# Attention by pairs of 64-row matmuls: scores of two key chunks side by side, the second product in two halves

## The chip, the cores and the metric

The kernel runs on one core of a Trainium2 chip. The metric is the device time of one execution in microseconds, the median of several. TensorE (PE in the profile) does the matmuls and loads its weights (PEld) beside them; ScalarE (ACT), VectorE (DVE) and GpSimd (POOL) do the rest of the arithmetic; SyncE (SP) issues most of the DMAs.

## What is computed

Three layers follow each other on 4 sequences of 3072 rows with 256 columns. The change touches the first alone.

```python
scores = (1 / S) * z @ z.T                # z: 3072 x 64 per sequence
attn = np.maximum(scores, 0.0) ** 2
x = u * (attn @ v)                        # v, u: 3072 x 256
h = x @ w_in;  x = (h - np.tanh(h)) @ w_out
k = np.maximum(mix_k(x) @ w_k, 0.0)
out = sigmoid(mix_r(x) @ w_r) * ((k * k) @ w_v)
```

## The kernel before

**Number format.** The matmuls take fp32r, a shortened fp32. Every operand is split into a high part h and the rest l, and a product is made of h·h, h·l and l·h (`PASSES`, line 605).

**Tiles and units.** Attention is cut into 24 tiles of 512 queries (`t`; batch `b` and group `g` are `divmod(t, 6)`). A tile has 12 units, each of two key chunks of 128 keys. A unit's scores go to a work tile `w_A` in PSUM (128 x 2 x 512), ScalarE applies relu (line 632) and square (633) and rounds the result to h (89), VectorE takes the rest l (92), and the second product `acc_A` (line 880) multiplies h and l by v. Since z @ z.T is symmetric, a block of scores that was made in an earlier tile of the same batch is not made again: VectorE turns it (661), SyncE stores it (669, `at`), and it is loaded later (695, `b`) as a reused unit. Of the 288 units 168 are fresh and 120 reused; group 0 has 12 fresh ones per tile, group 5 has two. The table `pairs` (line 647) says in which place of a tile a fresh ("f") and a reused ("r") unit stand.

**Scores.** z has 64 columns and TensorE's contraction has 128 rows. Before, `z1` holds h of z on rows 0 to 63 and l on rows 64 to 127, and `z2` the same two swapped. A chunk's scores are two full matmuls into the same bank: z1 by z1 (h·h + l·l) and z1 by z2 (h·l + l·h). That is 4 matmuls per fresh unit.

**Second product.** Per unit 2 chunks x 2 column halves of v x 3 passes = 12 full matmuls, into two accumulator banks (`acc_A`, 128 x 512 each). Four banks exist with that tag, so two tiles can be under way. At the end of a tile VectorE multiplies each accumulator by u, straight from PSUM (line 1223), and the result is stored to `x1d`.

**Order.** All is written out by hand: unit n's scores, then the second product of unit n - 2 (`LAG` is 2), and so on. Each engine runs its own instructions strictly in the order in which they were written; all work between engines is tied by semaphores. Loads have a unit at which they are issued (`load`), other work (splitting weights, turning u, the multiply by u) is a list of steps that `run_steps` hands out between units, by a budget per unit (line 1394) and a last unit for each. After attention come the two feed-forward layers, which use TensorE with full 128-row matmuls throughout.

The profile names a buffer by its tag: `h_A`, `l_A` are the parts of a fresh unit, `h_t`, `l_t` those of a reused one, `z` is z1, z2 and, in the listings of order, q the queries.

Of the kernel before, what the change touches and what calls it, by code (L numbers as in the profile page):

```python
# [14 lines left out]
P = 128  # L15
# [4 lines left out]
def relu2_attention__tanh_ffn__channel_mix_kernel(  # L20
# [74 lines left out]
    zin, z1, z2, vraw, vs, uin, uT = {}, {}, {}, {}, {}, {}, {}  # L95

    def z_load(b, g):

        if (b, g) == (0, 2):
            t = p4(f"zin{b}_{g}", shape=(P, 32, 32))[:, :16]  # L100
        elif b:
            t = p2(f"zin{b}_{g}", F32R)
        else:
            t = p2(f"zin{b}_{g}").rearrange("p (k i) -> p k i", i=32)
        src = z[b, g * TB : (g + 1) * TB, :].rearrange("(k j) (a i) -> a j k i", j=32, i=32)
        o = t.bitcast(F32).rearrange("p (k i) -> p k i", i=32) if b else t
        for h in range(1 if b else P // DQ):
            for a in range(DQ // 32):
                q = nc.scalar if h and b == 0 and g < 2 else nc.sync
                q.dma_start(out=o[h * DQ + 32 * a : h * DQ + 32 * a + 32], in_=src[a])  # L110
        zin[b, g] = t

    def z_steps(b, g):
        st = {}

        def turn():
            a = zin.pop((b, g))
            st["t"] = t = scratch(f"zt{b}_{g}")[:, 0]
            st["w"] = w = p2(f"z1_{b}_{g}", F32R)
            nc.vector.transpose(out=t, in_=a.rearrange("p k i -> p (k i)"))  # L120

        def high():
            t, w = st["t"], st["w"]
            if b or g < 3:
                nc.vector.tensor_copy(w, t)
            else:
                copy_hi(w, t)
            if b == 0 and g == 0:
                z2[0] = p2("z2_0", F32R)
                copy_hi(z2[0][DQ:], t[DQ:])  # L130

        def low():
            t, w = st["t"], st["w"]
            sub_lo(w[DQ:], t[DQ:], w[DQ:])
            if b == 0 and g == 0:
                sub_lo(z2[0][:DQ], t[:DQ], w[:DQ])
            z1[b, g] = w

        if not b:
            return turn, high, low  # L140

        def half():

            a = zin[b, g]
            t = scratch(f"zt{b}_{g}")[:DQ, 0]
            st["w"] = w = p2(f"z1_{b}_{g}", F32R)
            nc.vector.transpose(out=t, in_=a[:DQ].bitcast(F32))
            nc.vector.tensor_copy(w[:DQ], t)
            sub_lo(a[:DQ], t, w[:DQ])
            z1[b, g] = w  # L150

        return [(1.7, half)]
# [478 lines left out]
    def square(a, w, sc):  # L631
        nc.scalar.activation(out=a, in_=w, func=ACTF.Relu, scale=sc)  # L632
        nc.scalar.activation(out=a, in_=a, func=ACTF.Square)  # L633

    def square_split(name, w, sc, high, beside, a=None):
        a = a or scratch(f"a_{name}")
        h, l = parts(name)
        square(a, w, sc)
# [7 lines left out]
    for g, order in enumerate(  # L646
        ("ffffffffffff", "ffffrfrfffff", "ffrffrffrffr", "frfrfrfrfrfr", "rfrrfrrfrrfr", "rrfrrrrrfrrr")
# [69 lines left out]
    def score(o, t, p, j, k):  # L717
        b, g = divmod(t, NG)
        kp = pairs[g][p]
        kc = kp // 2 * 4 + kp % 2 + 2 * j  # L720
        lhsT = z1[b, kc // 4][:, (kc % 4) * P : (kc % 4 + 1) * P]
        nc.tensor.matmul(o, lhsT, (z2[t], z1[b, g])[not k], start=not k, stop=bool(k))  # L722

    def opening(begin):
# [27 lines left out]
        def scores(n, o):  # L752
            for j in range(2):
                for k in range(2):
                    score(o[j], 0, n, j, k)
# [11 lines left out]
        for n, j, k in (  # L767
            (0, 0, 0), (0, 1, 0), (1, 0, 0), (0, 0, 1), (0, 1, 1), (1, 1, 0), (1, 0, 1), (1, 1, 1)
        ):
            score(o[n][j], 0, n, j, k)  # L770
# [11 lines left out]
        o = single(3)  # L782
        scores(3, o)
# [7 lines left out]
        square(x, w[1], scale)  # L791
        copy_hi(h, x)
# [7 lines left out]
        for n in (2, 3):  # L800
            a[n] = x = wide(n)
            if n == 2:
                square(x, w[2], scale)
                vh[1][0]()
            else:
                for j in range(2):
                    nc.scalar.activation(out=x[:, j], in_=o[j], func=ACTF.Relu, scale=scale)
                nc.scalar.activation(out=x, in_=x, func=ACTF.Square)
                vh[2][0]()
# [7 lines left out]
    def produce(unit):  # L817
# [3 lines left out]
        if n in turned:  # L821
            views, split[unit] = turned.pop(n)
            for hj, lj, xj in views:
                sub_lo(lj, xj, hj)
            return
        w = work(f"w_{name}")
        if kind == "A":
            b, g = divmod(t, NG)
            kp = pairs[g][p]
            for j in range(2):  # L830
                for k in range(2):
                    score(w[:, j], t, p, j, k)
            kept_on = (b, g, kp // 2) in kept

            def beside(a):
                run_steps(n)
                if kept_on and not later(n):
                    keep(n, b, g, kp, a)

            a = wide(n) if later(n) and kept_on else None  # L840
            split[unit] = square_split(
                name, w, scale,
                nc.vector.tensor_copy if not n // NP and n % 2 else copy_hi, beside, a,
            )
            if kept_on and later(n):
                keep(n, b, g, kp, a)

    def get_acc(kind, t):
        if (kind, t) not in acc:
            acc[kind, t] = [  # L850
                ps.tile([P, 512], F32, tag="acc", name=f"acc_{kind}{t}_{c}", bufs=2 * DC)
                for c in range(DC)
# [7 lines left out]
    def pieces_of(unit):  # L860
# [13 lines left out]
        elif unit in units[1 : NP - 1]:  # L874
            q = (0, 1, 2) if unit == units[2] else (0, 2, 1)
            order = [(j, c, n) for n in q for j in range(2) for c in range(DC)]

        def one(j, c, n):
            a, m = PASSES[n]
            nc.tensor.matmul(  # L880
                o[c],
                w[j][a][:, c * P : (c + 1) * P],
                s[m][:, j],
                start=p == 0 and j == 0 and n == 0,
                stop=p == last and j == 1 and n == 2,
            )
# [331 lines left out]

    def x1_steps(t):
        def f():  # L1220
            x, o = uT.pop(t), acc.pop(("A", t))
            for c in range(DC):
                nc.vector.tensor_tensor(out=x[:, c], in0=o[c], in1=x[:, c], op=ALU.mult)
# [33 lines left out]
    for t in range(NT):  # L1257
# [3 lines left out]
        if t:  # L1261
            load(t * NP - 5, z_swap, t)
        if t < NT - 1:
            task(t * NP + NP + LAG, t * NP + NP + LAG + 3, x1_steps, t)
    for b in range(1, B):
# [6 lines left out]
        for g in range(NG):  # L1272
# [3 lines left out]
            load(n + 6, z_below, b, g)  # L1276
# [110 lines left out]
    def run_steps(n):  # L1387
# [21 lines left out]
    with tc.manual_schedule():  # L1409
# [11 lines left out]
        for j in range(10):  # L1421
            for r in (slice(0, DQ), slice(DQ, P)) if 3 < j < 7 else (slice(0, P),):
                nc.tensor.matmul(  # L1423
                    idle[:, bool(r.start) if 3 < j < 7 else j % 2], zeros[r],
                    zeros[r].unsqueeze(1).broadcast_to([r.stop - r.start, 4, P]), start=True, stop=True,
# [87 lines left out]
```

## Time and profile before

| | us |
|---|---|
| median of 3 runs | 2478.32 (2478.29 to 2479.51) |
| the profiled execution | 2478.75 |
| its span, first to last instruction | 2477.0 |
| TensorE busy | 2469.6, 100% |
| VectorE, ScalarE busy | 1955.1 (79%), 1889.0 (76%) |
| second product of attention, share of the chain | 32% |
| scores of attention, share of the chain | 6% |

The span holds 31131 instructions. Times in rows are us from the span's start. A matmul's row gives its length to the last result, and the next one starts before that; the time that a matmul costs is the distance between two starts. In rows of the timeline that stand for several instructions, x2 means that two follow each other in one row with one start and one total length. In the rows of stretches, (x884) is the number of instructions that touch the stretch.

### The profile page before, as it was taken

What the parts mean: (1) busy time and instruction counts of PE and PEld (TensorE: products, weight loads), DVE (VectorE), ACT (ScalarE), POOL (GpSimd) and SP (SyncE); (2) the same over time, 40 slices, a digit from 0 to 9 for tenths busy, and PEclk for the clock granted to TensorE, in tenths of its full rate; (3) what the DMA queues carried; (4) which work ended last, traced back from release to release, by engine and by line L of the source; (5) the groups of instructions that cost most, each with busy time, mean ns of one, the idle gap of its engine ahead of it and who ended that gap; (6) DMA issues with size and microseconds to landing.
All of it is one profiled execution on the core that took longest, in us unless ns stands there. A gap on an engine that the chain in (4) does not pass through costs nothing.

```text
span 2477.0 us, 31131 instructions
## 1 busy us (share of the span) xinstructions
PE 2469.6 (100%) x10873; PEld 2040.1 (82%) x10873; DVE 1955.1 (79%) x2723; ACT 1889.0 (76%) x2516; POOL 242.7 (10%) x314
## 2 busy tenths in 40 slices
PE   9999999999999999999999999999999999999998
PEld 7888888888888888888888888888888888888887
DVE  8887888787888868777777777777778778878877
ACT  8766876787678766777777777778777988888886
POOL 0000000000000000022132222222222000000200
PEclk9999999999999999999999999999999999999999
DMA  7799579768967991155665556545667454445733
GB/s 200 230 224 221 191 209 248 200 198 214 244 191 224 271 231 69 47 109 109 145 134 122 101 111 132 125 96 109 135 127 166 137 128 128 105 125 133 164 106 71
DMA packets 442670, 385.87 MB, mean 156 GB/s; under 512 B 263952, under 2 KB 349968, under 8 KB 442512
## 3 DMA queue, kind: packets, MB, share of 16 engines
q1 hardware_dynamic: 390288, 307.58, 44.0%
q0 software_dynamic: 45888, 75.51, 18.3%
q8 instruction: 85, 1.39, 0.2%
q10 hardware_dynamic: 6336, 0.79, 0.2%
q14 instruction: 73, 0.60, 0.1%
HBM read 226.23 MB, written 199.48 MB: 172 GB/s over the span
## 4 chain that ended last, share of the span: by engine, by line
PE 100%; DVE 0%; issue 0%; POOL 0%; DVEq 0%; POOLq 0%
PE acc_A L880 32%; PE acc_H L936 21%; PE wa L899 16%; PE we L899 12%; PE acc_K L936 10%; PE w_A L722 6%; PE wa_r L899 1%; PE we_q L899 1%; PE we_r L899 0%; PE idle L1423 0%; DVE ot L1211 0%; DVE sg L1202 0%; POOL zeros L1418 0%; DVEq L1202 0%; POOLq L1500 0%
## 5 line engine op out<-in xcount | busy, mean ns | idle before, releaser
L880 PE MATMUL acc_A<-h_A,v 128*128 128x512 f32 x1344 | 433.1, 389 | 0.1
L632 ACT ACTIVATE a_A<-w_A 128x1024 f32<-128x1024 f32 (+1 forms) x168 | 171.6, 1021 | 181.6 <-PE w_A L722 181.3
L880 PE MATMUL acc_A<-h_t,v 128*128 128x512 f32 x960 | 310.0, 389 | 0.0
L880 PEld LDWEIGHTS acc_A<-h_A,v 128*128 128x128 f32 x1344 | 252.1, 188 | 52.7 <-issue 0.5
L936 PE MATMUL acc_H<-h_Hy,w_out 128*128 128x512 f32 x768 | 263.8, 389 | 0.0
L880 PE MATMUL acc_A<-l_A,v 128*128 128x512 f32 x672 | 256.4, 389 | 0.0
L92 DVE TENSOR_TENSOR l_A<-a_A,h_A 128x1024 fp32r<-128x1024 f32 (+1 forms) x169 | 201.3, 1191 | 64.6 <-ACT h_A L89 63.9
L936 PE MATMUL acc_H<-h_Hx,w_out 128*128 128x512 f32 x768 | 252.1, 389 | 0.0
L899 PE MATMUL wa<-xo_T,w_in 128*128 128x512 f32 x864 | 242.8, 389 | 0.0
L661 DVE STREAM_TRANSPOSE k<-a_A 128x512 f32<-128x512 f32 x240 | 156.1, 689 | 78.9 <-ACT a_A L633 78.4
L880 PEld LDWEIGHTS acc_A<-h_t,v 128*128 128x128 f32 x960 | 180.2, 188 | 37.4
L1002 DVE TENSOR_TENSOR r<-we,r 128x512 f32<-128x512 f32 x144 | 99.5, 691 | 126.1 <-PE we L899 84.8
L1162 POOL DMA_DIRECT2D mixd<-far x48 | 48.7, 1014 | 1511.4 <-ACT far L1159 1496.2
L1036 DVE TENSOR_TENSOR rc<-we,rc 128x512 f32<-128x512 f32 x144 | 99.3, 689 | 119.0 <-PE we L899 83.5
L899 PEld LDWEIGHTS wa<-xo_T,w_in 128*128 128x128 f32 x864 | 162.1, 188 | 34.1 <-DVE rc L1036 0.4
L880 PE MATMUL acc_A<-l_t,v 128*128 128x512 f32 x480 | 186.7, 389 | 0.0
L633 ACT ACTIVATE a_A<-a_A 128x1024 f32<-128x1024 f32 (+1 forms) x168 | 177.4, 1056 | 5.3
L92 DVE TENSOR_TENSOR l_Hy<-g_H,h_Hy 128x1024 fp32r<-128x1024 f32 x144 | 175.5, 1219 | 7.3 <-ACT h_Hy L89 4.6
L89 ACT ACTIVATE h_t<-b 128x512 fp32r<-128x512 f32 x240 | 137.1, 619 | 56.1 <-PE acc_A L880 56.1
L92 DVE TENSOR_TENSOR l_Hx<-g_H,h_Hx 128x1024 fp32r<-128x1024 f32 (+1 forms) x145 | 175.3, 1209 | 3.5 <-ACT h_Hx L89 2.5
L909 ACT ACTIVATE g_H<-rc 128x1024 f32<-128x1024 f32 x96 | 101.9, 1061 | 96.4 <-DVE rc L1036 95.4
L89 ACT ACTIVATE h_A<-a_A 128x1024 fp32r<-128x1024 f32 x161 | 170.6, 1060 | 4.6
(254 smaller groups left out, 5744.3 us busy)
## 6 DMA issues: line engine op xcount, KB each, us to landing
at<-k SPq DMA_DIRECT2D x120, 512.0 KB, 3.7
b<-at SPq DMA_DIRECT2D x240, 256.0 KB, 6.5
timed<-mixd POOLq DMA_DIRECT2D x144, 256.0 KB, 5.3
mixd<-own SPq DMA_DIRECT2D x96, 256.0 KB, 2.1
mx_T<-timed SPq DMA_DIRECT2D x96, 256.0 KB, 4.6
mx_B<-mixd SPq DMA_DIRECT2D x72, 256.0 KB, 4.6
uin<-in_u_dram SPq DMA_DIRECT2D x192, 64.0 KB, 2.7
x1d<-uT SPq DMA_DIRECT2D x24, 512.0 KB, 4.6
```

The lines of the kernel that those rows point to most:

```text
L89: nc.scalar.activation(out=o, in_=i, func=ACTF.Copy)
L92: nc.vector.tensor_tensor(out=o, in0=i, in1=hi.bitcast(F32), op=ALU.subtract)
L632: nc.scalar.activation(out=a, in_=w, func=ACTF.Relu, scale=sc)
L633: nc.scalar.activation(out=a, in_=a, func=ACTF.Square)
L661: nc.vector.transpose(out=t[:, :, :, c].rearrange("p b a j -> p a b j"), in_=a[:, c].rearrange("p (a b i) -> p a b i", a=4, b=4),)
L722: nc.tensor.matmul(o, lhsT, (z2[t], z1[b, g])[not k], start=not k, stop=bool(k))
L880: nc.tensor.matmul(o[c], w[j][a][:, c * P : (c + 1) * P], s[m][:, j], start=p == 0 and j == 0 and n == 0, stop=p == last and j == 1 and n ...
L899: nc.tensor.matmul(o, w[l], x[m], start=first and k == 0, stop=last and k == 2, skip_group_check=True,)
L909: nc.scalar.activation(out=g, in_=h, func=ACTF.Tanh)
L936: nc.tensor.matmul(o[c], w[a][:, f % 4, c * P : (c + 1) * P], hp[n, half, t][m], start=bool(first and k == 0), stop=bool(last and k == 2),)
L1002: nc.vector.tensor_tensor(out=r1, in0=e, in1=r1, op=ALU.add)
L1036: nc.vector.tensor_tensor(out=rc[:, k], in0=x, in1=rc[:, k], op=ALU.add)
```

## The change

- Scores take three passes (h·h, h·l, l·h), each of two 64-row matmuls: key chunk j has its 64 columns of z on rows 64 j to 64 j + 63, with its own bank of `w_A`. `keys` holds h and l of a group's keys laid out so, and `asks` the queries with the same 64 columns on both row halves. `ask` fills the queries by eight DMAs from `keys`, where `z_swap` had two; `z_below` is gone.
- The second product goes in 64-row matmuls as well: rows 0 to 63 into accumulators 2 and 3, rows 64 to 127 into accumulators 0 and 1. Only the last two units of attention stay whole. In a tile's first and last unit the column halves follow each other (c outside).
- At the end of a tile `x1_add` copies accumulators 0 and 1 to SBUF on ScalarE and adds 2 and 3 on VectorE, before the multiply by u. For the scores of the unit at that place ScalarE's copies stand behind the relu and behind the square.
- `produce` is split: `scores` ahead of the second product of unit n - 2, the rest behind it. Two rows of `pairs` are rearranged, the budget of `run_steps` is 1.4 lower at the second unit of a tile, and the warm-up matmuls are all halves.

```diff
         def turn():
             a = zin.pop((b, g))
-            st["t"] = t = scratch(f"zt{b}_{g}")[:, 0]
-            st["w"] = w = p2(f"z1_{b}_{g}", F32R)
+            st["t"] = t = scratch(f"zt{b}_{g}")[:, 0, :n]
+            if n == 512:
+                w = asks[0] = [p2(f"q0_{l}", F32R) for l in range(2)]
+            else:
+                w = p2(f"z_{b}_{g}", F32R).rearrange("p (l n) -> p l n", l=2)
+                w = [w[:, l] for l in range(2)]
+            st["w"] = w
...
-    def z_below(b, g):
-        a = zin.pop((b, g))
-        nc.sync.dma_start(out=z1[b, g][DQ:].bitcast(F32), in_=a[:DQ].bitcast(F32))
-
-    def z_swap(t):
+    def ask(t):
+
         b, g = divmod(t, NG)
-        w = p2(f"z2_{t}", F32R)
-        nc.sync.dma_start(out=w[:DQ].bitcast(F32), in_=z1[b, g][DQ:].bitcast(F32))
-        nc.sync.dma_start(out=w[DQ:].bitcast(F32), in_=z1[b, g][:DQ].bitcast(F32))
-        z2[t] = w
+        w = asks[t] = [p2(f"q{t}_{l}", F32R) for l in range(2)]
+        for l in range(2):
+            for d in range(2):
+                for h in range(2):
+                    nc.sync.dma_start(
+                        out=w[l][d * DQ : (d + 1) * DQ, h * 256 : (h + 1) * 256].bitcast(F32),
+                        in_=keys[b, g][l][h * DQ : (h + 1) * DQ].bitcast(F32),
+                    )
...
-    def score(o, t, p, j, k):
+    def score(o, t, p, k):
+
         b, g = divmod(t, NG)
         kp = pairs[g][p]
-        kc = kp // 2 * 4 + kp % 2 + 2 * j
-        lhsT = z1[b, kc // 4][:, (kc % 4) * P : (kc % 4 + 1) * P]
-        nc.tensor.matmul(o, lhsT, (z2[t], z1[b, g])[not k], start=not k, stop=bool(k))
+        for j in range(2):
+            r = slice(j * DQ, (j + 1) * DQ)
+            n = kp % 2 + (2 * j if (b, kp // 2) == (0, 0) else 0)
+            lhsT = keys[b, kp // 2][PASSES[k][0]][r, n * P : (n + 1) * P]
+            nc.tensor.matmul(o[j], lhsT, asks[t][PASSES[k][1]][r], start=k == 0, stop=k == 2)
...
+        elif p in (0, last):
+            order = [(j, c, n) for c in range(DC) for n in range(3) for j in range(2)]
+        whole = at[unit] >= NA - LAG
 
         def one(j, c, n):
+
             a, m = PASSES[n]
-            nc.tensor.matmul(
-                o[c],
-                w[j][a][:, c * P : (c + 1) * P],
-                s[m][:, j],
-                start=p == 0 and j == 0 and n == 0,
-                stop=p == last and j == 1 and n == 2,
-            )
+            for r in (slice(0, P),) if whole else (slice(0, DQ), slice(DQ, P)):
+                nc.tensor.matmul(
+                    o[c if r.start else DC + c],
+                    w[j][a][r, c * P : (c + 1) * P],
+                    s[m][r, j],
...
+    def x1_add(t):
+
+        x = added[t] = scratch(f"xs{t}")
+        o = acc["A", t] if t == NT - 1 else acc.pop(("A", t))
+
+        def one(c):
+            nc.scalar.activation(out=x[:, c], in_=o[c], func=ACTF.Copy)
+            if t < NT - 1:
+                nc.vector.tensor_tensor(out=x[:, c], in0=o[DC + c], in1=x[:, c], op=ALU.add)
+
+        return [lambda c=c: one(c) for c in range(DC)]
...
-            load(t * NP - 5, z_swap, t)
+            load(t * NP - 5, ask, t)
...
+            left -= 1.4 if q == LAG - 1 else 0.0
...
-            produce(units[n])
+            w = scores(units[n])
             consume(units[n - LAG])
+            ends_now = n == NA - 1 or n % NP == LAG - 1 and n > NP
+            produce(units[n], w, x1_add((n - LAG) // NP) if ends_now else ())
```

TensorE at the end of tile 6, before: the scores of unit 1 of tile 7 (`w_A7_1`), then the first six of the twelve matmuls of the last unit of tile 6.

```order
L722 MATMUL w_A7_1_2721<-z1_1_1_1255 128x512
L722 MATMUL w_A7_1_2721<-z2_7_2528,z1_1_1_1255 128x512
L722 MATMUL w_A7_1_2721<-z1_1_1_1255 128x512
L722 MATMUL w_A7_1_2721<-z2_7_2528,z1_1_1_1255 128x512
L880 MATMUL acc_A6_0_2393<-h_A6_11_2661,v1_5_2477 128x512
L880 MATMUL acc_A6_0_2393<-l_A6_11_2662,v1_5_2477 128x512
L880 MATMUL acc_A6_0_2393<-h_A6_11_2661,v1_5_2477 128x512
L880 MATMUL acc_A6_1_2394<-h_A6_11_2661,v1_5_2477 128x512
L880 MATMUL acc_A6_1_2394<-l_A6_11_2662,v1_5_2477 128x512
L880 MATMUL acc_A6_1_2394<-h_A6_11_2661,v1_5_2477 128x512
```

The same place in the changed kernel; the number behind `acc_A6` is the accumulator.

```order
L724 MATMUL w_A7_1_3918<-q7_0_3631,z_1_1_1720 128x512 x2
L724 MATMUL w_A7_1_3918<-q7_1_3632,z_1_1_1720 128x512 x2
L724 MATMUL w_A7_1_3918<-q7_0_3631,z_1_1_1720 128x512 x2
L881 MATMUL acc_A6_2_3413<-h_A6_11_3855,v1_5_3809 128x512
L881 MATMUL acc_A6_0_3411<-h_A6_11_3855,v1_5_3809 128x512
L881 MATMUL acc_A6_2_3413<-h_A6_11_3855,v1_5_3809 128x512
L881 MATMUL acc_A6_0_3411<-h_A6_11_3855,v1_5_3809 128x512
L881 MATMUL acc_A6_2_3413<-l_A6_11_3856,v1_5_3809 128x512
L881 MATMUL acc_A6_0_3411<-l_A6_11_3856,v1_5_3809 128x512
L881 MATMUL acc_A6_2_3413<-l_A6_11_3856,v1_5_3809 128x512
L881 MATMUL acc_A6_0_3411<-l_A6_11_3856,v1_5_3809 128x512
```

Four full score matmuls became three pairs of halves, and each full matmul of the second product a pair that alternates between two accumulators. The listing has 10873 matmuls before and 14648 after.

ScalarE at that place, before: relu, square and rounding of units 1 and 2 of tile 7.

```order
L632 ACTIVATE a_A7_1_2726<-w_A7_1_2721 128x1024
L633 ACTIVATE a_A7_1_2726<-a_A7_1_2726 128x1024
L89 ACTIVATE h_A7_1_2727<-a_A7_1_2726 128x1024
L632 ACTIVATE a_A7_2_2757<-w_A7_2_2752 128x1024
L633 ACTIVATE a_A7_2_2757<-a_A7_2_2757 128x1024
```

In the changed kernel (`xs6` is the SBUF tile that takes tile 6's accumulators):

```order
L627 ACTIVATE a_A7_1_3950<-w_A7_1_3918 128x1024
L1229 ACTIVATE xs6_3949<-acc_A6_0_3411 128x512
L630 ACTIVATE a_A7_1_3950<-a_A7_1_3950 128x1024
L1229 ACTIVATE xs6_3949<-acc_A6_1_3412 128x512
L89 ACTIVATE h_A7_1_3951<-a_A7_1_3950 128x1024
L627 ACTIVATE a_A7_2_3996<-w_A7_2_3961 128x1024
```

Two copies of accumulators now stand between the steps of unit 1; each waits for TensorE's last matmul into its bank, and VectorE's two additions stand behind them on VectorE.

## Rows read from the trace of the kernel before

**Rows 1.** The page: busy time of the engines, and the chain that ended last.

```profile
PE 2469.6 (100%) x10873; PEld 2040.1 (82%) x10873; DVE 1955.1 (79%) x2723; ACT 1889.0 (76%) x2516; POOL 242.7 (10%) x314
PE 100%; DVE 0%; issue 0%; POOL 0%; DVEq 0%; POOLq 0%
```

**Rows 2.** The whole span, matmuls of line 880, then of 722: busy us (xcount).

```profile
0.00:2477.00 2477.00, 811.42 (x3456) 648.25 (x3456) 1.00 0.63 156
...
0.00:2477.00 2477.00, 179.89 (x672) 126.52 (x672) 1.00 0.63 156
```

**Rows 3.** The chain that ended last, in order of time: start us, us.

```profile
207.81 16.32 PE acc_A L880 x72
```

**Rows 4.** Timeline of TensorE's warm-up, six moments, then its weight load: start us, us.

```profile
2.02 0.63 PE L1423 MATMUL idle<-zeros 128*128 128x512 f32 x1
2.44 0.63 PE L1423 MATMUL idle<-zeros 128*128 128x512 f32 x1
3.00 0.79 PE L1423 MATMUL idle<-zeros 64*128 64x512 f32 x2
3.60 0.63 PE L1423 MATMUL idle<-zeros 64*128 64x512 f32 x2
4.02 0.63 PE L1423 MATMUL idle<-zeros 64*128 64x512 f32 x2
4.58 0.79 PE L1423 MATMUL idle<-zeros 128*128 128x512 f32 x1
5.17 0.63 PE L1423 MATMUL idle<-zeros 128*128 128x512 f32 x1
...
3.60 0.33 PEld L1423 LDWEIGHTS idle<-zeros 64*128 64x128 f32 x2
```

**Rows 5.** Warm-up stretch: busy PE, PEld, DVE, ACT, POOL (xcount), clock, DMA share, GB/s.

```profile
0.00:6.00 6.00, 5.00 (x13) 2.92 (x14) 1.96 (x4) 1.91 (x2) 0.41 (x5) 1.00 0.80 144
```

**Rows 6.** Timeline of ScalarE in tile 6, all fresh units: start us, us, what.

```profile
244.83 1.01 ACT L632 ACTIVATE a_A<-w_A 128x1024 f32<-128x1024 f32 x1
...
247.94 1.01 ACT L632 ACTIVATE a_A<-w_A 128x1024 f32<-128x1024 f32 x1
...
251.37 1.03 ACT L632 ACTIVATE a_A<-w_A 128x1024 f32<-128x1024 f32 x1 [0.24 <-PE w_A L722]
...
255.00 1.03 ACT L632 ACTIVATE a_A<-w_A 128x1024 f32<-128x1024 f32 x1 [0.41 <-PE w_A L722]
...
257.02 1.99 ACT L89 ACTIVATE v<-vr 128x1024 fp32r<-128x1024 f32 x2
...
259.87 1.00 ACT L632 ACTIVATE a_A<-w_A 128x1024 f32<-128x1024 f32 x1
```

**Rows 7.** The same tile: TensorE at two moments, then VectorE.

```profile
251.17 0.39 PE L880 MATMUL acc_A<-h_A,v 128*128 128x512 f32 x1
...
258.65 0.39 PE L880 MATMUL acc_A<-l_A,v 128*128 128x512 f32 x1
...
254.75 1.18 DVE L92 TENSOR_TENSOR l_A<-a_A,h_A 128x1024 fp32r<-128x1024 f32 x1
```

**Rows 8.** Stretches: tile 6 (group 0) and tile 10 (group 4), columns as in rows 5.

```profile
243.92:287.44 43.52, 43.52 (x194) 36.04 (x192) 38.48 (x52) 40.05 (x39) 0.00 (x0) 1.00 0.61 195
...
405.30:441.57 36.27, 36.27 (x162) 30.03 (x160) 30.31 (x47) 21.01 (x29) 0.00 (x0) 1.00 1.04 251
```

**Rows 9.** Durations elsewhere: PSUM copy, PSUM addition (mean ns), then DMA issues and landings.

```profile
L905 ACT ACTIVATE r<-wa 128x512 f32<-128x512 f32 x141 | 84.1, 597 | 21.6 <-PE wa L899 14.1 <-DMA mixd<-x2r 0.9
L1002 DVE TENSOR_TENSOR r<-we,r 128x512 f32<-128x512 f32 x141 | 97.4, 691 | 125.6 <-PE we L899 84.5 <-ACT r L905 39.1 <-DMA timed<-mixd 1.0
...
L161 SPq DMA_DIRECT2D z<-z x23: 461/467/966, 24.0 to 890.5; - x23
DMA to landing us min/median/max: 2.2/4.6/9.7
...
DMA to landing us min/median/max: 3.2/6.5/11.1
```

More of the change, by code (lines that the diff above doesn't have):

```diff
@@ L134, in low, with whole @@
[L134 to L137, printed above, removed]
+            sub_lo(st["w"][1], st["t"], st["w"][0])
+            keys[b, g] = st["w"]
+        def whole():
+            turn()
+            high()
+            low()
         if not b:
             return turn, high, low
[L142 to L150, printed above, removed]
@@ L752, in scores @@
         def scores(n, o):
-            for j in range(2):
-                for k in range(2):
-                    score(o[j], 0, n, j, k)
+            for k in range(3):
+                score(o, 0, n, k)
         def double(n):
@@ L766, in opening @@
         o = single(0), double(1)
[L767 to L770, printed above, removed]
+        for n, k in ((0, 0), (1, 0), (0, 1), (0, 2), (1, 1), (1, 2)):
+            score(o[n], 0, n, k)
         a[0], a[1] = scratch("a_A0_0"), scratch("a_A0_1")
@@ L791, in opening @@
         square(x, w[1], scale)
+        scores(3, double(3))
         copy_hi(h, x)
@@ L801, in opening @@
             a[n] = x = wide(n)
[L802 to L809, printed above, removed]
+            square(x, w[n], scale)
+            vh[n - 1][0]()
             split[units[n]] = h, l = parts(f"A0_{n}")
@@ L815, in opening, with scores, produce @@
             keep(n, 0, 0, pairs[0][n], x)
-    def produce(unit):
+    def scores(unit):
+        if at[unit] not in turned:
+            w = work(f"w_{unit[0]}{unit[1]}_{unit[2]}")
+            for k in range(3):
+                score([w[:, j] for j in range(2)], unit[1], unit[2], k)
+            return w
+    def produce(unit, w, adds):
         kind, t, p = unit
@@ L824, in produce, with beside @@
                 sub_lo(lj, xj, hj)
+            for f in adds:
+                f()
             return
[L826 to L843, printed above, removed]
-            )
-            if kept_on and later(n):
-                keep(n, b, g, kp, a)
+        b, g = divmod(t, NG)
+        kp = pairs[g][p]
+        kept_on = (b, g, kp // 2) in kept
+        def beside(a):
+            run_steps(n)
+            if kept_on and not later(n):
+                keep(n, b, g, kp, a)
+        a = wide(n) if later(n) and kept_on else None
+        split[unit] = square_split(
+            name, w, scale,
+            nc.vector.tensor_copy if not n // NP and n % 2 else copy_hi, beside, a, adds,
+        )
+        if kept_on and later(n):
+            keep(n, b, g, kp, a)
     def get_acc(kind, t):
@@ L1421, in relu2_attention__tanh_ffn__channel_mix_kernel @@
         for j in range(10):
[L1422 removed]
+            for r in range(2):
+                x = zeros[r * DQ : (r + 1) * DQ]
                 nc.tensor.matmul(
[L1424 to L1425 removed]
+                    idle[:, r], x, x.unsqueeze(1).broadcast_to([DQ, 4, P]), start=True, stop=True
                 )
```

61 lines of the change are left out of this document (33 added, 28 removed).

## The prediction

> **What bounds the kernel now.** I read the page first: TensorE is busy all of its 2477.0 us and the chain that ended last is 100% TensorE [rows 1]. So only something that takes work from TensorE can pay, and every wait that the change makes for TensorE costs its full length. The attention stage holds 3456 matmuls of the second product and 672 of the scores [rows 2]; the chain of waits shows them end to end, 72 in 16.32 us, which is 226.7 ns each, with nothing between [rows 3]. A fresh unit is 4 + 12 matmuls (3.63 us), a reused one 12 (2.72 us). The 168 fresh units are 672 / 4.
>
> What no long stretch of this trace shows is two 64-row matmuls side by side at full speed. But the warm-up at the start holds six of them, between full ones, and that is the next view [rows 4]. Last, who stands just behind TensorE: ScalarE and VectorE in a tile of twelve fresh units, and the DMA engines in tile 4 of a batch [rows 6 to 8].
>
> **What a pair costs.** In the warm-up the full matmuls start 0.42 us apart (2.02, 2.44). The halves start two at a time, at 3.00, 3.60 and 4.02: two halves on separate rows and into separate banks take one slot, and the two together last 0.63 us, as long as one alone. Their two weight loads run together too, 0.33 us both (3.60). Going from full to halves and back costs some 0.13 us more on each crossing and again in the slot after it (2.44 to 3.00, 3.00 to 3.60, 4.02 to 4.58, 4.58 to 5.17) [rows 4]. In the changed kernel all matmuls from the warm-up to the last two attention units are halves, so there is one crossing instead of some 300; that is 0.3 us, left out.
>
> These rows are at the lower of the two clock levels: 512 columns in 0.427 us is 1.2 per ns, though the row of the granted clock reads 1.00 there as it does everywhere [rows 5]. At the higher level 512 columns at 2.4 GHz would be 213.3 ns, and a slot measures 226.7: 13.3 ns more, which the slow stretch doesn't show. How a pair pays these 13.3 ns is not in the trace. The bounds are: the pair hides them (213.3 ns), the pair pays them once as a full matmul does (226.7), each half pays its own in turn (240), or even the weight loads go one after another (two of 188 ns, 376; 2040.1 us for 10873 loads is 188 [rows 1]). I take 226.7, because the two matmuls of a pair last 0.63 us together, to the 0.01 us of the rows [rows 4]: were 13 ns of a start something that the halves take in turn, it would be 0.64.
>
> **The change part by part.**
> - Scores: three passes of one pair instead of four full matmuls. 168 units x 1 slot x 226.7 ns = **38.1 us less** on the chain.
> - Second product: 3432 of 3456 matmuls become pairs (the last 24 stay whole). At 226.7 ns a pair: nothing. With the 504 score pairs there are 3936 pairs, so each nanosecond that a pair costs more is 3.9 us.
> - Accumulators: a tile now needs four banks, and there are four, so the next tile's first product waits until ScalarE has copied one half out and VectorE has added the other. I follow a boundary with a fresh unit from the end of its scores (0): the last unit's first column half ends at 6 slots = 1.36, its second at 2.72, the next scores at 3.40, and then the new tile needs the first two banks at 3.40, the second two at 4.76. ScalarE: relu starts 0.20 after the scores (251.37 after 251.17 [rows 6, 7]) and ends at 1.23; copy 0 at 1.56 to 2.16 (0.60 from PSUM [rows 9]), square to 3.2, copy 1 to 3.85. VectorE adds in 0.69 [rows 9]: done at 2.9 and 4.6. Spare: 0.5 and 0.15 us. Queued behind the two waiting copies on ScalarE are the square and the rounding of the same unit, which are not used until two units later. So most boundaries cost nothing, some a few tenths; 23 x 0.13 = **3 us**.
> - ScalarE, where its cover is thinnest, a tile of twelve fresh units: TensorE's time falls from 43.52 to 12 x 15 x 226.7 ns = 40.8. ScalarE was busy 40.05 there [rows 8] and gets two copies (1.2): 41.3. From the starts it is 3.11 per unit (244.83 to 247.94) and 0.88 for each v conversion (255.00 to 259.87 holds two) [rows 6]: 12 x 3.11 + 4 x 0.88 + 1.2 = 42.0. It falls 0.5 to 1.2 us behind in such a tile. Its lead: the unit whose relu began at 251.37 has its low part at 254.75 + 1.18 = 255.93 and is needed at 258.65 [rows 6, 7], 2.7 us; two shorter score groups between make that 2.3. The lag fits in; nothing on the chain. VectorE: 38.48 of 43.52 [rows 8] + two adds (1.4), and one wide multiply for two narrow ones: about 39.8 of 40.8, also inside; the z preparation gets half as wide, which only helps.
> - DMA: eight quarter-size loads per tile for the queries where two were, and the copy of z's low half is gone: 156 issues more in all (1297 and 1453 in the two programs) on SP's queue at 0.47 us each, where loads stand in order; they are asked for five units (13.6 us or more) ahead and land in 4.6 [rows 9]. In tile 4 of a batch the DMA engines are already at 1.04 of their time with 251 GB/s [rows 8]: there 256 KB more is 1.0 us, and TensorE's 0.9 us less takes away as much again, 2 us per tile by which a reused block can come later; it takes 6.5 us (11.1 at most) of its 13.6 [rows 9]. That cover is thin in tiles 3 to 5 alone; I put **2 us** for the four batches (0 if it holds, 25 if all twelve tiles lose 2.1).
> - The opening: z's rounding is one piece instead of two halves, so scores can start at once when the warm-up ends; ScalarE then still waits for v. Nothing.
>
> Sum: -38.1 + 3 + 2 = -33.1 us. The profiled execution took 2478.75 (span 2477.0), 0.4 above the median 2478.3; from the median, **2445 us** (2436 to 2457: boundaries at 0 to 0.4 us, DMA at 0 to 4, a pair within 1 ns of 226.7).
>
> **A rule that speaks against it.** The warm-up rows give a pair the slot of one matmul [rows 4]. The Trainium skill, "TensorE: Matmul & The Clock Gate", section "Measured speedup vs the span model", says that packed tiles cost about 4 ns for each tile beyond the first, and measured 3.07 rather than 4 for four row tiles. Estimates from that page: 4 ns a pair is 15.7 us more, 2461; its 77% of the ideal, if it held for two tiles, would be 68 ns a pair and a much slower kernel. The rows show neither at the lower clock, and no row shows the higher.
>
> **The rivals.**
> - *A start that the halves take one after the other in part* (the rule above): the rows leave room for 0.00 to 0.01 us per pair; at the middle, 5 ns, it is 19.7 us, 2465. Chance 0.03.
> - *Each half pays its own 13.3 ns (the other side).* Place: every one of the 3936 pairs at full clock; price 52.5 us; it outweighs the 33 saved from 8.4 ns a pair on. Time 2445 + 52.5 = 2498. For it: the excess exists at full speed alone, so the slow warm-up could have hidden it. Against it: the pairs start together. Chance 0.13; paid in part, so that the time stays within 0.2%, 2473 to 2483: 0.04; weight loads in turn (149 ns a pair, 588 us): 0.02.
> - *The accumulators come back late.* Spare at the second two banks is only 0.15 us; if ScalarE stands half a microsecond behind at every boundary, 23 x 0.7 = 16 instead of 3: 2458. For it: ScalarE was at 92% in fresh tiles [rows 8]. Against it: in the other tiles it was near 60%. Chance 0.09.
> - *Reused blocks come late in tiles 3 to 5*: 25 us instead of 2: 2468. For it the DMA share of 1.04 [rows 8], against it 13.6 us of lead. Chance 0.05.
> - *The pair hides the excess*: 3936 x 13.3 less, 2393. No row for it but that halves are independent. Chance 0.05.
>
> **How the numbers follow.** Forecast 0.59 (2445), the pair's start 0.03, accumulators 0.09, DMA 0.05, hidden excess 0.05: faster 0.81. Half-paid excess: same 0.04. Excess paid in full 0.13 and loads in turn 0.02: slower 0.15. A measurement here can tell about 0.2% (5 us). Range: from the forecast's low end 2436 to 2483 holds 0.59 + 0.03 + 0.09 + 0.05 + 0.04 = 0.80.
>
> **What would show it.** In the profile after: TensorE's count is 14648; two score rows with the same start, and pair after pair 226 to 227 ns apart in the middle of a tile (240 would be the slower rival, 230 the rule's). A tile of twelve fresh units takes 40.8 us plus what its boundary waits. Idle time of TensorE before the first product of a tile, released by VectorE's add, is the accumulators; idle before a product of reused units, with ScalarE waiting for a DMA, is the blocks. The stages after attention keep their times. Wrong would be above all a pair's slot other than 226.7.

## The result and the profile after

The changed kernel takes **2494.53 us** (2491.75 to 2496.21, 4 runs) against 2478.43 (2478.29 to 2479.51, 4 runs) for the kernel before: a ratio of 1.0063 (95%: 1.0045 to 1.0080). It is 0.6% slower, where 2445 was forecast, and lies above the whole range.

The page of the changed kernel: busy times; the chain that ended last, by engine; two groups of second products (busy us, mean ns | idle before).

```profile
PE 2455.3 (98%) x14648; PEld 2026.6 (81%) x14648; DVE 1968.1 (79%) x2746; ACT 1906.8 (76%) x2562; POOL 242.4 (10%) x314
...
PE 87%; DVE 4%; DMA 3%; ACT 2%; SPq 1%; issue 1%; DVEq 0%; ACTq 0%
...
L881 PE MATMUL acc_A<-h_t,v 64*128 64x512 f32 (+1 forms) x1904 | 352.7, 393 | 16.6 <-ACT xs L1229 8.4
...
L881 PE MATMUL acc_A<-l_A,v 64*128 64x512 f32 x1344 | 307.1, 392 | 11.2 <-DVE l_A L92 11.1
```

TensorE has less to do (2455.3 us against 2469.6 [rows 1]), but the chain, which was 100% TensorE, now has 13% of other things in it. Stretches of the changed kernel: tiles 6, 10 and 11, and everything behind attention (columns as in rows 5).

```profile
246.20:287.90 41.70, 41.70 (x364) 33.42 (x362) 37.70 (x47) 40.76 (x43) 0.00 (x0) 1.00 0.63 206
...
407.10:446.90 39.80, 35.76 (x316) 29.24 (x312) 25.71 (x39) 23.10 (x32) 0.00 (x0) 1.00 0.85 202
446.90:489.40 42.50, 40.94 (x314) 31.88 (x316) 30.72 (x49) 22.56 (x31) 0.00 (x0) 0.88 0.88 220
...
965.50:2494.00 1528.50, 1521.84 (x6707) 1257.43 (x6705) 1182.96 (x1611) 1198.36 (x1726) 241.20 (x308) 1.00 0.53 117
```

Tile 6, all fresh, is 1.8 us shorter than before, where 2.7 were forecast; tile 10, mostly reused, went from 36.27 [rows 8] to 39.80, and tile 11 from 36.3 to 42.5. Behind attention almost nothing changed (1527.6 us before). So the loss is in attention, which ends 16 us later instead of 33 earlier. The waits of TensorE there, in us, times, longest:

```profile
PE acc_A L881 <- DVE l_A L92: 11.1, 9, 2.3
PE acc_A L881 <- DVE xs L1231: 9.6, 5, 4.5
PE acc_A L881 <- ACT xs L1229: 8.4, 3, 4.0
```

These are 29 us; counted by tiles (the table further down) the loss is 52. A bit more than half of the other 23, 13 us, are 62 slots at a lower clock behind the waits, as the TensorE rows from 296.68 on will show; most of the rest are longer slots at full clock right after a wait.

**One of the two largest stalls, read backwards** (the other, at 687 in tile 16, has rows of the same kind). At 447 the first product of tile 11 waits for the copies and additions of tile 10's sums. ScalarE, then VectorE there (start us, us, what [idle before]):

```profile
444.15 2.19 ACT L89 ACTIVATE h_t<-b 128x512 fp32r<-128x512 f32 x4 [8.59 <-DMA b<-at]
446.24 1.06 ACT L1229 ACTIVATE xs<-acc_A 128x512 f32<-128x512 f32 x2
...
446.14 0.45 DVE L127 STREAM_TRANSPOSE zt<-zin 128x256 f32<-128x256 f32 x1 [9.02 <-DMA zin<-in_z_dram]
...
451.10 1.28 DVE L1231 TENSOR_TENSOR xs<-acc_A,xs 128x512 f32<-128x512 f32 x2
```

The copies (line 1229) were not late by themselves: they stand on ScalarE behind the rounding of a reused block that had not landed, and the additions stand on VectorE behind a z that had not landed and, after it, behind low parts of the late blocks and three steps of a weight conversion. The block and z were asked for late, as SyncE's queue in the changed kernel shows (start us, us that the issues took, line, what, count):

```profile
419.73 10.07 SPq L207 DMA_DIRECT2D uin<-in_u_dram  x8
...
430.38 4.95 SPq L155 DMA_DIRECT2D q<-z  x8
435.43 2.04 SPq L694 DMA_DIRECT2D b<-at  x4
437.51 0.45 SPq L164 DMA_DIRECT2D vr<-in_v_dram  x1
438.08 2.51 SPq L108 DMA_DIRECT2D zin<-in_z_dram  x4
```

And the same place in the kernel before:

```profile
412.84 8.69 SPq L212 DMA_DIRECT2D uin<-in_u_dram  x8
421.63 0.47 SPq L161 DMA_DIRECT2D z<-z  x1
422.14 0.60 SPq L162 DMA_DIRECT2D z<-z  x1
422.84 2.04 SPq L695 DMA_DIRECT2D b<-at  x4
...
425.46 1.13 SPq L110 DMA_DIRECT2D zin<-in_z_dram  x2
```

SyncE issues one load after the other, and all wait their turn. The loads of u hold it for 4 to 10 us a tile in both kernels. Behind them the two query copies took 1.1 us; the eight take 4.95, and z's four 2.51 instead of 1.13. The block behind the queries is issued 12.6 us later in the span, though tile 10 itself began only 1.8 later: the queue came to these loads of u 6.9 us later already, 1.4 are added by them, 0.5 by a weight store and 3.8 by the queries. From the start of its tile that is 28.3 us instead of 17.5, and a block is asked for only five units (13.6 us and more) ahead. The blocks are not slower, they are asked for later: from issue to landing they take a median of 6.5 us before and 6.3 after (count, KB each, us):

```profile
b<-at SPq DMA_DIRECT2D x240, 256.0 KB, 6.5
...
b<-at SPq DMA_DIRECT2D x240, 256.0 KB, 6.3
```

**A stall of the other kind.** VectorE and then TensorE at the third unit of tile 7, changed kernel:

```profile
290.18 0.42 DVE L267 TENSOR_SCALAR c_in<-cw_in 128x512 int32<-128x512 int32 x1
...
293.61 0.69 DVE L286 TENSOR_TENSOR cw_in<-cw_in 128x512 f32<-128x512 f32 x1
294.22 1.29 DVE L660 STREAM_TRANSPOSE k<-a_A 128x512 f32<-128x512 f32 x2
295.44 1.18 DVE L92 TENSOR_TENSOR l_A<-a_A,h_A 128x1024 fp32r<-128x1024 f32 x1
...
293.75 0.64 PE L881 MATMUL acc_A<-h_A,v 64*128 64x512 f32 x4
296.68 0.50 PE L881 MATMUL acc_A<-l_A,v 64*128 64x512 f32 x2 [2.29 <-DVE l_A L92]
...
297.73 1.06 PE L881 MATMUL acc_A<-h_A,v 64*128 64x512 f32 x4
```

Seven steps of a weight conversion (4 us) stand ahead of the low part that TensorE needs. The budget's cut of 1.4 at a tile's second unit had put them off until they were due. After the stall four halves take 1.06 us, not 0.64: the clock fell. Stretches before, at and after it:

```profile
288.70:294.40 5.70, 5.69 (x51) 4.95 (x48) 5.27 (x10) 5.57 (x7) 0.00 (x0) 1.00 0.08 12
296.60:299.40 2.80, 2.72 (x16) 2.19 (x18) 2.80 (x5) 0.00 (x0) 0.00 (x0) 0.69 0.64 263
```

TensorE had worked without a break before the wait; behind it the granted clock is 0.69 on average, partly the lower level of 1.2 GHz. A pair then starts every 0.427 us instead of 0.227, for some eight pairs, so a wait of 2.3 us costs some 3.9; all of tile 7 loses 4.2.

### The profile page after: what moved, and what is told of

It reads as the page before. It is cut to its first block, busy times and chain, and to the rows that moved or that the text cites. A ratio compares the mean times of both kernels' runs of the same rounds, so it can differ in the third digit from the quotient of the medians.

```text
span 2494.3 us, 38956 instructions
## 1 busy us (share of the span) xinstructions
PE 2455.3 (98%) x14648; PEld 2026.6 (81%) x14648; DVE 1968.1 (79%) x2746; ACT 1906.8 (76%) x2562; POOL 242.4 (10%) x314
## 4 chain that ended last, share of the span: by engine, by line
PE 87%; DVE 4%; DMA 3%; ACT 2%; SPq 1%; issue 1%; DVEq 0%; ACTq 0%
PE acc_A L881 23%; PE acc_H L938 21%; PE wa L901 16%; PE we L901 12%; PE acc_K L938 10%; PE w_A L724 3%; DMA b<-at 2%; PE wa_r L901 1%; DVE l_A L92 1%; DVE l_t L92 1%; PE we_q L901 1%; SPq L207 1%; ACT a_A L630 1%; DVE k L660 1%; ACT a_A L627 0%
## 5 line engine op out<-in xcount | busy, mean ns | idle before, releaser
L881 PE MATMUL acc_A<-h_A,v 64*128 64x512 f32 x2688 | 466.6, 390 | 2.4 <-DVE xs L1231 1.4
L881 PE MATMUL acc_A<-h_t,v 64*128 64x512 f32 (+1 forms) x1904 | 352.7, 393 | 16.6 <-ACT xs L1229 8.4
L881 PEld LDWEIGHTS acc_A<-h_A,v 64*128 64x128 f32 x2688 | 312.5, 186 | 54.8 <-DVE xs L1231 4.6
L881 PE MATMUL acc_A<-l_A,v 64*128 64x512 f32 x1344 | 307.1, 392 | 11.2 <-DVE l_A L92 11.1
L881 PEld LDWEIGHTS acc_A<-h_t,v 64*128 64x128 f32 (+1 forms) x1904 | 256.1, 188 | 56.6 <-DVE xs L1231 10.9
L881 PE MATMUL acc_A<-l_t,v 64*128 64x512 f32 (+1 forms) x952 | 255.1, 393 | 0.5 <-DVE l_t L92 0.5
L881 PEld LDWEIGHTS acc_A<-l_A,v 64*128 64x128 f32 x1344 | 172.0, 186 | 42.0 <-DVE l_A L92 17.6
```

Of the source, the lines that this page charges most:

```text
L881: nc.tensor.matmul(o[c if r.start else DC + c], w[j][a][r, c * P : (c + 1) * P], s[m][r, j], start=p == 0 and j == 0 and n == 0, stop=p == ...
```

## The experiments

The version before took 2478.3 to 2478.7 us beside all of them.

**The queue.** The first edit moves the changed kernel's query loads to GpSimd's queue.

```diff
-                    nc.sync.dma_start(
+                    nc.gpsimd.dma_start(
                         out=w[l][d * DQ : (d + 1) * DQ, h * 256 : (h + 1) * 256].bitcast(F32),
```

> The changed kernel with the eight query loads per tile issued on GpSimd's queue instead of SyncE's; same bytes, same packets. Theory (SyncE's queue issues the reused blocks too late in tiles 4 and 5 of a batch): the 4.95 us that the eight loads hold the queue go, blocks come up to 5 us earlier, the waits at the ends of tiles 4, 10 and 16 shrink by most of their 4 to 7 us each, and the time falls by 15 to 25 us to about 2470 to 2480. Rival (the DMA engines' bandwidth is the limit there, since they move the same bytes): no change, 2490 to 2497.

2473.19 (ratio to before 0.9978, 0.9968 to 0.9987): 21.3 us less than the changed kernel, as the theory had it. By tiles the loss falls from 52 to 31, and 19 of these 21 us are in groups 4 and 5, where most units are reused. The block of the stall above is issued 23.1 us after its tile's start, 5.2 sooner:

```profile
424.85 1.98 SPq L694 DMA_DIRECT2D b<-at  x4
```

The same bytes are still moved, so it was the place in SyncE's queue and not bandwidth.

**The budget**: `left -= 1.4 if q == LAG - 1 else 0.0` taken out of `run_steps`.

> The changed kernel without the 1.4 us that run_steps gets less at the second unit of a tile. Theory (the cut puts steps off until their last unit forces them out together, as the weight steps of 4 us in unit 2 of tile 7): the stalls of 4.2 to 4.4 us in tiles 2, 7 and 13 shrink, 8 to 13 us less, about 2484. Rival (the cut is needed, the additions of the accumulators come late without it): new waits before a tile's first products, and no gain or a loss.

2486.42 (1.0031, 1.0020 to 1.0041): 8.1 us less, as expected. Tiles 2, 7 and 13 lose 1.6 to 1.7 us each instead of 4.2 to 4.4.

**Both, and z's loads** from the second batch on also on GpSimd's queue:

```diff
-                q = nc.scalar if h and b == 0 and g < 2 else nc.sync
+                q = nc.scalar if h and b == 0 and g < 2 else nc.gpsimd if b else nc.sync
```

> Query loads and, from the second batch on, the z loads on GpSimd's queue, and no budget cut. If both theories hold and nothing else limits, the pairs' 38 us show: 2478 - 38 + about 10 to 15 for boundaries and what is left, 2450 to 2456. If bandwidth is the limit: about as e2 alone.

2457.96 (0.9917, 0.9902 to 0.9931), 2 us above the range expected. Taking z's loads back to SyncE splits the sum:

> e3_both_and_z with z's loads back on SyncE's queue: that is the changed kernel with two edits, queries asked for on GpSimd's queue, and no 1.4 us taken from the step budget. The query loads alone gave -21.3 us, the budget alone -8.1, all three edits -36.6, so 7.2 us belong to z's loads or to the two edits helping each other. Theory Z (z's loads still stand behind the loads of u in SyncE's queue: with the queries moved alone, tile 11 still lost 7.8 us, VectorE waiting there): 2463 to 2466, the 7 us in tile 11. Rival (the edits help each other, z is indifferent): 2457 to 2459.

2468.66 (0.9959, 0.9944 to 0.9974), so taking z's loads off SyncE's queue is worth 10.7 us once the queries are gone from it; what their cut from two into four adds alone was not measured. The direction of theory Z held, its size (7 us) and its place did not: tile 5 is 6.9 us longer, tile 16 3.7, and tile 11 only 1.2.

**The loads without the halves.** The kernel before, with its two query copies replaced by eight, which move 512 KB a tile instead of 256, as in the changed kernel:

```diff
-        nc.sync.dma_start(out=w[:DQ].bitcast(F32), in_=z1[b, g][DQ:].bitcast(F32))
-        nc.sync.dma_start(out=w[DQ:].bitcast(F32), in_=z1[b, g][:DQ].bitcast(F32))
+        for k in range(2):
+            for d in range(2):
+                for h in range(2):
+                    cols = slice(h * 256, (h + 1) * 256)
+                    nc.sync.dma_start(out=w[d * DQ : (d + 1) * DQ, cols].bitcast(F32),
+                        in_=z1[b, g][(1 - d) * DQ : (2 - d) * DQ, cols].bitcast(F32))
```

> The kernel before with its query loads cut as in the changed kernel: eight loads of 64 x 256 on SyncE's queue where two of 64 x 512 were, each piece loaded twice, 512 KB per tile. All matmuls are the old ones. Theory (the queue is at its limit in tiles 3 to 5): blocks come later there by up to 4 us per tile, the smallest margins (about 1 to 3 us in the first batch) go, 2 to 10 us slower, 2480 to 2488. Rival (only the shorter units make the loads late): no change, 2478 to 2480.

2501.49 (1.0090, 1.0075 to 1.0105): 23 us more, far over the 2 to 10 of the theory; the rival gave none. The matmuls and the accumulators are those of before, so the loads alone make a loss of this size, with no copies or additions at a tile's end. Its waits of ScalarE for blocks (us, times, longest), of which the kernel before has none:

```profile
ACT h_t L89 <- DMA b<-at: 37.3, 11, 7.3
```

**Relief alone.** The kernel before with its query copies, low-half copy and z loads on GpSimd's queue; and, on top of the 2458 version, the loads of u there too:

> The kernel before, with its two query copies and one low-half copy per tile, and z's loads from the second batch on, asked for on GpSimd's queue instead of SyncE's, as in e3_both_and_z; matmuls, accumulators and tables as before. Theory A (SyncE's queue hurts only with the change's eight loads, so relieving it is no gain without them): 2478 within 2 us. Rival (the kernel before lost time in that queue too, and e3's gain over it is the queue's): 2458 to 2470. If A holds, the whole gain of e3 over the kernel before comes from the halves.

> Base is e3_both_and_z (2458.0), with the eight loads of u per tile, which hold SyncE's queue for some 10 us, on GpSimd's queue as well. Theory A (what is left in the queue still delays blocks): a tile in which blocks are short of margin gains, but the base's trace shows tiles 3 to 5, 9 to 11, 15 to 17 and 21, 22 already at 0 to 0.9 us lost, so at most 3 us less: 2455 to 2458. Rival (GpSimd's queue becomes the crowded one and the query loads come late): 2460 to 2480.

2478.84 (1.0001, 0.9991 to 1.0010): no gain without the halves. The kernel before loses 0.4 us in its tiles in all, so there was no wait to save, and the gain of 2458 over 2478 comes from the slots that the halves save. And 2457.07 (0.9912, 0.9897 to 0.9927): the loads of u gain nothing more.

**Scores alone in halves**, the second product whole, into two accumulators without copies or additions (base: the 2458 version):

```diff
-            for r in (slice(0, P),) if whole else (slice(0, DQ), slice(DQ, P)):
-                nc.tensor.matmul(o[c if r.start else DC + c], w[j][a][r, c * P : (c + 1) * P], s[m][r, j],
+            nc.tensor.matmul(o[c], w[j][a][:, c * P : (c + 1) * P], s[m][:, j],
```

> Base is e3_both_and_z (2458.0); here only the scores stay in halves, and the second product goes back to whole 128-row matmuls into two accumulators (no copy and no addition at a tile's end). Theory S (going from whole to half matmuls costs something on each crossing, as in the warm-up rows, where a crossing cost 0.13 us and the slot after it as much again): 168 fresh units, two crossings each, 0.13 to 0.28 us a crossing at the low clock, perhaps half at the high one: 22 to 94 us more than the base, less the 14 us that the base loses at its boundaries: 2465 to 2540. Rival (crossings are free at full clock, so the second product need not have been cut): 2440 to 2446, the forecast's own time. In the trace the first matmul after a crossing tells: 226.7 ns after the one before it (rival), more (S).

2512.97 (1.0138, 1.0122 to 1.0155). Its chain is 99% TensorE; two units of a fresh tile:

```profile
262.49 0.39 PE L877 MATMUL acc_A<-h_A,v 128*128 128x512 f32 x1
262.81 0.96 PE L724 MATMUL w_A<-q,z 64*128 64x512 f32 x6
263.70 0.50 PE L877 MATMUL acc_A<-h_A,v 128*128 128x512 f32 x1
...
266.64 0.97 PE L724 MATMUL w_A<-q,z 64*128 64x512 f32 x6
```

From 262.81 to 266.64 a unit takes 3.83 us, 15 slots would be 3.40: 0.43 us for going to halves and back. For 168 units that is 72 us, less 38 saved: 34, and 34.3 is what it is slower. So the second product had to be cut as well. The Trainium skill, "TensorEngine Tiling (Array Packing)", section "Key Properties", says that a change of tiling mode drains TensorE; this run is in line with that, at 0.22 us a change.

**What is left of 2458: VectorE at the start of fresh tiles.** There tiles 2, 7, 13, 14, 18 and 20 still lose 1.5 to 1.8 us each, nearly all in a wait of TensorE for a low part (us, times, longest; tile 8, which the expectation names too, loses 0.4):

```profile
PE acc_A L881 <- DVE l_A L92: 8.2, 7, 1.5
```

First the steps of the boundary's unit were moved behind its low part (`if not adds: run_steps(n)` ahead of it, `if adds: run_steps(n)` behind):

> Base is e3_both_and_z (2458.0), which loses 1.4 to 1.8 us at the second unit of tiles 2, 7, 8, 13, 14, 18 and 20, where TensorE waits for VectorE's low part, behind six steps of weight conversion (3 us) and the tile's additions. Here the steps of the one unit in which a tile's sums are copied and added are issued behind the unit's low part instead of ahead of it; nothing else moves. Theory B (the order on VectorE at the boundary makes the stall): the seven stalls go, 10 to 11 us less, 2447 to 2449. Rival (the additions themselves, which wait for ScalarE's copies, make it): the low part comes at most as early as the copies let it, less than 3 us gained of the 14, 2455 to 2458.

2457.60 (0.9914, 0.9899 to 0.9928): nothing. The stall moved from the second unit to the third, whose low part then stood behind the same steps. So B fell as it was put, and on this version less work was tried: the multiply by u on GpSimd (`nc.gpsimd.tensor_tensor`, its store on that queue), then left out altogether.

> Base is e6_steps_after_low (2457.6). Its trace shows that moving the conversion steps only moved the stall: TensorE now waits at the third unit of tiles 2, 7, 8, 13, 14, 18, 19 and 20 (0.6 to 2.0 us, released by VectorE's low part), some 9 us in all, and VectorE has hardly an idle moment there but the 0.7 to 0.9 us in which each addition stands waiting for ScalarE's copy. Here a tile's closing multiply (1.2 us on VectorE, in those very units) and its store go to GpSimd; the last tile's stay. Theory V (VectorE is short of time in the first units after a boundary, in whatever order they come): 1.2 us less to do, so of the eight stalls 0.6 to 1.2 us each go, 6 to 8 us less: 2450 to 2452. Rival (what counts is only the order, copies and additions behind one another): no change, 2456 to 2459. A mishap would be a multiply on GpSimd that stands behind query loads and slows VectorE beside it.

> Base is e6_steps_after_low (2457.6); the closing multiply with u (1.2 us on VectorE a tile) is left out for all tiles but the last, so the sums are stored unmultiplied; everything else stays. It splits the result of e9 (2478.6), where the multiply on GpSimd took 2.4 us and the VectorE subtraction beside it 3.31 instead of 1.2 us. Theory V (VectorE is short of time in the first units after a boundary; e9 failed because GpSimd's multiply holds VectorE up): 0.6 to 1.2 us less at each of eight stalls, 2449 to 2452. Rival (VectorE's amount of work there doesn't matter): 2456 to 2459.

On GpSimd 2478.60 (0.9999, 0.9989 to 1.0009), 21 us worse; left out 2455.53 (0.9909, 0.9893 to 0.9926), 2.1 us better at most. GpSimd's row and VectorE's beside it (tile 7) say why; in eleven of the 23 tiles the subtraction beside the multiply takes 3.3 us or more:

```profile
286.53 2.40 POOL L1246 TENSOR_TENSOR uT<-xs,uT 128x1024 f32<-128x1024 f32 x1 [34.46 <-DVE xs L1234]
...
286.70 3.31 DVE L92 TENSOR_TENSOR l_A<-a_A,h_A 128x1024 fp32r<-128x1024 f32 x1 [0.26 <-ACT h_A L89]
```

Theory V (too little time) lost most of its ground: 1.2 us less work per boundary gave 2.1 us of the 6 to 8 that it asked. Next the steps were kept out of the first units, and the conversions due later: first out of four units (`q < 4`) with six units' grace (`+ 8`), then, as in the diff, out of the second and third with two.

```diff
             left -= 0.3 if later(n) else 1.0 if j < 0 else 1.1 if j > 0 else 0.0
+            if n >= NP and q in (1, 2) and t % NG < 3:
+                left = min(left, 0.0)
...
-        task(k, k + (c1 - c0) // len(halves) + 2, c_steps, *x)
+        task(k, k + (c1 - c0) // len(halves) + 4, c_steps, *x)
```

> Base is e6_steps_after_low (2457.6). In tiles 0 to 2 of a batch, where units are mostly fresh, none of the planner's steps (weight conversions, multiply, z) is taken in a tile's first four units unless it is due, and the conversions are due six units later, so that they aren't due there. Ahead of the third unit's low part VectorE then has one transpose instead of six conversion steps, a transpose and nothing else. Theory V: the eight stalls at the third unit (0.6 to 2.0 us, 9 us in all) go, 2447 to 2450. Rival W (the waits of the additions for ScalarE's copies, 1.7 us a boundary, are what can't be made up): half of them stay, 2452 to 2455. If the conversions only pile up later in the tile, as the budget cut did: 2456 or more.

> Base is e6_steps_after_low (2457.6). e12 (2463.4) freed the first units of a tile from VectorE's steps and lost more further back: its stalls at tiles 1, 2, 7, 13 and 19 are gone, and new ones stand behind heaps of six to eight conversion steps that had come due (tile 20: 3.5 us behind eight). Here only the second and third unit are kept free, and the conversions come due two units later than in e6 instead of six, so that heaps of five are gone in the order. Theory P (the stalls are heaps of steps on VectorE wherever the planner puts them, the boundary only makes them shorter lived): 3 to 8 us less, 2450 to 2455. Rival V (the first units of a fresh tile don't have the time, however steps lie): 2456 to 2459.

2463.39 (0.9938, 0.9924 to 0.9953) and **2449.96** (0.9885, 0.9869 to 0.9902). The first cleared the boundaries and piled conversions up behind them (in tile 20 TensorE waited 3.3 us behind eight steps); the second, at the low end of what theory P gave, has little of either left, and TensorE's waits for low parts are down to 2.7 us. Its two edits were not tried apart. Those waits (us, times, longest), then its stretches for tiles 6, 7 and 8:

```profile
PE acc_A L884 <- DVE l_A L92: 2.7, 3, 1.6
...
237.70:278.50 40.80, 40.80 (x364) 40.80 (x362) 36.95 (x47) 39.44 (x41) 6.45 (x12) 1.00 0.64 217
278.50:317.90 39.40, 39.40 (x351) 39.40 (x349) 34.53 (x49) 34.21 (x37) 4.07 (x7) 1.00 0.67 198
317.90:355.30 37.40, 37.40 (x333) 37.40 (x330) 33.30 (x49) 29.28 (x35) 4.76 (x9) 1.00 0.82 230
```

40.80 is 12 x 15 slots of 226.7 ns: no loss at all in tile 6, copies and additions included. Last, all conversions were put into tiles 2 to 5 (`places = [k for k in range(c0, c1) if 26 <= k % (NG * NP) < 67]`, due after 8 units):

> Base is e6_steps_after_low (2457.6). All weight conversions (25 of them, some 5 us of VectorE each) are placed in tiles 2 to 5 of a batch, where units are mostly reused and VectorE is busy 72 to 90%, none in the fresh tiles 0 and 1. Theory P: the stalls of tiles 7, 8, 13, 14, 18, 19 and 20 go, 2447 to 2452. Rival D (the tiles 3 to 5 have the DMA engines at 0.92 to 1.04 of their time, and the loads of the weights on SyncE's queue make blocks late there): 2458 to 2475, with ScalarE waiting for blocks.

2476.38 (0.9989, 0.9980 to 0.9999). The stalls of tiles 7, 8, 13, 14, 19 and 20 are gone, as P has it, but the time is just above D's range. D explains a part: ScalarE waits for blocks in four places, 12.5 us. The two longest waits of TensorE, 3.5 us each in tiles 4 and 10, are heaps again: in tile 10 VectorE runs ten conversion steps in a row, from 428.81 to 434.46, ahead of a low part. How the loss divides between the two is left open.

## Why the prediction was wrong

Time lost per group of tiles, us: the tile's length from first product to first product, less 15 slots per fresh unit and 12 per reused one; sums over the four batches, without the last tile (before: nearly 0 in all).

| tiles | changed | 2458 version | 2450 version |
|---|---|---|---|
| group 0 | 3.8 | 2.4 | 0.9 |
| group 1 | 9.9 | 4.3 | 0.4 |
| group 2 | 7.3 | 5.8 | 2.1 |
| group 3 | 2.7 | 1.3 | 2.3 |
| group 4 | 9.9 | 0.4 | 0.0 |
| group 5 | 18.5 | 1.1 | 2.1 |
| all | 52 | 15 | 8 |

- **A pair at 226.7 ns, scores 38.1 us less: right.** Of the 3804 slots in the tiles of the table 3535 are 226 or 227 ns long, and whole tiles come out at the forecast 40.8 once nothing else is late (43.52 before [rows 8]). In most pairs the second half starts 3 to 4 ns behind the first, yet the slot does not grow. If the rule of about 4 ns per tile (the Trainium skill, "TensorE: Matmul & The Clock Gate", section "Measured speedup vs the span model") is added to every slot, an estimate for a pair is 230.7 ns and for the tile 41.5 us. The trace agrees inside a pair and not from pair to pair. The rival that each half pays its own 13.3 ns names a time near the result, 2498, but only by chance: its mechanism is absent.
- **DMA, 2 us: the step that failed.** "They are asked for five units (13.6 us or more) ahead and land in 4.6" looked at the new loads alone. The reused blocks were priced by the DMA engines' share, 2 us a tile out of a spare of 7; their place in SyncE's queue behind the new loads was not priced, and z, which is in four loads now, not at all. ("Quarter-size" is a slip too: a query load is 64 KB where it was 128, half the size.) In the trace a block is issued 10.8 us later in its tile, and its lead is gone. Off SyncE's queue the queries' loads are worth 21.3 us and then z's 10.7, 32 in all. The rival "reused blocks come late" had the right effect and place, at a chance of 0.05, but its 25 us were worked out from the DMA engines' share and not from the queue; that they lie near 21.3 is partly luck.
- **Accumulators, 3 us: right in itself.** With nothing else late, a boundary costs 0 in most tiles and about 0.35 in those of group 3 (2458 version). What the step missed is that the copies and additions stand in order on ScalarE and VectorE, so a block or z that is late there now stops TensorE too, which has no second set of banks, as at 447. How much that adds is not shown: with the accumulators of before the query loads cost 23 us as well.
- **ScalarE and VectorE in fresh tiles, "inside": wrong in the small.** The sum over the tile fits, as the 2450 version shows; the steps come in heaps, and the lead is only two units. The budget's cut was not priced at all. It and the heaps are worth 12.5 us (2468.7 without the cut against 2473.2, and 2450.0 against 2458.0).
- **A wait costs more than its length**: counted slot by slot, the 52 us are 33 in slots that hold a wait, 13 in 62 slots at the lower clock behind waits, and 6 in slots that are longer at full clock, most of them the restarts. The fall of the clock stood nowhere in the sum.

So 2494.5 - 21.3 - 10.7 - 12.5 = 2450.0, in the order in which the edits were added; the parts depend on it (the budget's cut is worth 8.1 us alone and 4.5 after the queries' loads). That is 5 us over the forecast: the table still has 8 where the forecast had put 5, and the other 2 lie outside the tiles of the table.

## What to carry to other kernels

When a change adds DMAs to a queue, price not when they land but what stands behind them in the queue, and the spare time of each of those. When a change takes away double buffering, a wait on the engines that free the buffer can become a wait of the bound engine, so look there first for work that is held up behind something that has not come. And an average of 90% busy says nothing about a lead of two units: look for the longest run of other work ahead of what is needed next.

## What was unexpected of the hardware

- Two 64-row matmuls of 512 columns cost one slot of 226.7 ns at full clock, and going between halves and whole matmuls 0.22 us each way (scores alone in halves: 3.83 us a unit for 3.40).
- Moving eight issues per tile from one queue to another was worth 21 us. The Trainium skill, "DMA: Bandwidth & Descriptors", section "Issuing engines are not separate DMA queues", calls the sequencer's time that this saves usually small relative to the DMA itself. It is smaller here too (a query load takes 0.62 us to issue and 2.4 to land), but it was time ahead of other loads, and it added up.
- A GpSimd multiply of two SBUF tensors (2.40 us) made VectorE's subtraction of two SBUF tensors beside it take 3.31 us instead of 1.2. The Trainium skill, "GPSIMD Engine Reference", section "Specifications", names this contention for VectorE instructions with two SBUF inputs; this run agrees. Instructions with one input were held up as well: a cast of 128x256 beside it took 2.26 us, 0.29 elsewhere.
- A TensorE wait of 2.3 us was followed by a granted clock of 0.69 over the next 2.8 us.
